# k^T v on quarters of the TensorE array, with a new order of the front

## The chip, the cores and the metric

The kernel runs on one core of a Trainium2 chip. The metric is the device time of one execution in microseconds, the median of three runs. The kernel takes float32 inputs and returns a float32 output; inside, most products work on 16-bit floats and sum in 32 bits.

## The reference

Linear attention with an ELU feature map feeds a layer of eight experts, whose routing weights come from eight rounds of Sinkhorn scaling. Shapes: batch 8, 8 heads, 576 positions, head size 64; 4608 tokens of 512 features; 8 experts with 1024 hidden features.

```
phi(x) = where(x > 0, x, exp(x) - 1) + 1
kv  = einsum('bhsd,bhse->bhde', phi(k), v)      # the products that are changed
z   = sum over s of phi(k)
num = einsum('bhsd,bhde->bhse', phi(q), kv)
den = einsum('bhsd,bhd->bhs', phi(q), z) + 1e-6
x   = num / den, heads side by side: (4608, 512)

P = exp(x @ w_gate - max); eight times: P /= row sums; P /= column sums; P *= N / E
out = sum over e of P[:, e] * (relu(x @ w1[e]) @ w2[e])
```

## The kernel before

**A plan of tasks.** The kernel doesn't emit its instructions as it goes through the loops. It adds tasks to a plan (`_Plan.add`), each with an engine, a duration, the tasks that it depends on, and the buffers that it takes from pools and hands back. `_Plan.run` then emits the tasks. Where a list of (task, engine) pairs is given, that list decides the order; after its end the planner picks by start time and priority. The list is the string `_FRONT`: a number is a task, the letter its engine (p TensorE, a ScalarE, d VectorE, g GpSimd, s SyncE, m a transfer, n nothing). A task that two engines could do (`{"dve": 0.43, "act": 0.37}`) is given to one of them by the letter. Each engine works through its own instructions in the order in which they were emitted.

**The front.** `_FRONT` covers the attention of all 8 batches and, between its pieces, the work of the first expert that can already be done. Attention goes by step: one step is one batch and one group of four heads, 16 steps in all. A step holds the 128 partitions as two halves of 64: the lower half has heads of one pair, the upper of the other; `r` is the head within the pair, `j` runs over 9 positions of 64 rows. For each step `att`

- loads k, q and v (line 380: GpSimd's queue, but for the very first k, which goes by SyncE's), 3 buffers of each; the planner reckons with 8 loads under way in GpSimd's queue;
- computes phi(k) into `t` (exponential on ScalarE, L390; two operations on VectorE, L394 and L398), and phi(q) into `tq` in the same way (L447, L450, L454);
- multiplies `t` with v on TensorE into `kv_ps` (`f_kv`, L413) - this is what the change touches. The tile `vv` holds v of head 0, a block of ones, and v of head 1, so that one product gives kv and z together;
- copies the useful part of `kv_ps` into `kvz` (L340 on ScalarE, L342 on VectorE, one copy for each head of the pair);
- transposes `tq` on TensorE (L439), copies the result (`qpT`), multiplies it with `kvz` for the denominators (`att`, L470) and the numerators (`num_ps`, L470), and forms the quotient by logarithm and exponential (L483, L488 on ScalarE) and a product on VectorE (L498) into `xT`.

Of the 128 x 192 result of a half-array product, rows of head 0 use the columns of v0 and ones, rows of head 1 the columns of ones and v1.

**Around it.** At the start TensorE has 46 products on zeros (`warm`, L590) to fill its waits. The first expert's first layer writes `hq` (L684), its second `ye` (L932), both by groups of four products of 512 columns. After every second batch `logits` (L515) computes the gate's values, 36 products of 8 columns. When the last are there, the Sinkhorn rounds run on VectorE (L541 to L565) with one small product on TensorE in each (`R`, L556). Beside them, blocks of sums and differences of `xT` (L726 to L731, on VectorE or GpSimd, into `acc` and later into `xst`) and of weights (`W`, L982) are made, from which later units compute with seven products in place of eight (L810, L1050); they are stored to `xd` by SyncE's queue, and an `xst` buffer is free again when its store has landed. For experts 1 to 7 the order of TensorE's work is fixed by a chain of dependencies.

## Time and profile before

| what | value |
|---|---|
| time, median of 3 runs | 964.44 us (964.11 to 965.62) |
| time of the profiled execution | 967.64 us |
| its span, first to last instruction | 965.6 us |
| busy TensorE, VectorE, ScalarE, GpSimd | 98%, 81%, 60%, 19% |
| mean granted TensorE clock | 0.997 |
| 18 products of a kv step (L413) | 16 steps of 0.92 us or a little less |
| group L413 | x288, 243 ns each, 14.7 us busy |

The profile is one execution, taken apart by engine. A line of the timeline or of the chain gives start and length in microseconds, the engine, the line of the kernel and the tile written and read. TensorE's instructions are pipelined: the length of a single product contains its latency, so the distance between two starts says more than the length. The profiled execution is 2.0 us longer than its span, and 3.2 us above the median of the runs.

### The profile page before, as it was taken

Reading aid. Unit: us, or ns where it says so; the run is one execution under the profiler, and the core shown is the slowest. Engines: PE = TensorE matmul, PEld = TensorE weight load, DVE = VectorE, ACT = ScalarE, POOL = GpSimd, SP = SyncE. Lnnn points to the kernel's source line nnn. Section 1 sums busy time; section 2 is a strip of 40 time slices with the busy share of each in tenths; the row PEclk is TensorE's granted clock in tenths of the full one; section 3 lists DMA queues with packets and bytes.
Section 4 is the critical chain, followed back from the end, with each engine's and each line's share of the span. In section 5 each row is a group of like instructions: output and inputs, shape, how many; then the busy total and the mean of one; then the engine's idle time right before and its main releaser. Section 6 shows DMA issues by size and latency. Waiting matters only on the chain.

```text
span 965.6 us, 21108 instructions
## 1 busy us (share of the span) xinstructions
PE 950.3 (98%) x8576; PEld 805.2 (83%) x8576; DVE 782.0 (81%) x1474; ACT 579.3 (60%) x1031; POOL 184.6 (19%) x238
## 2 busy tenths in 40 slices
PE   7999999999999999999999999999999999999998
PEld 4555568888888888888888888888888888888886
DVE  6899899778888788878887888878887888877775
ACT  6898856666655555555555555555555555555553
POOL 6435021452111121111112111111112111111110
PEclk9999999999999999999999999999999999999999
DMA  9999382225323352262226322272226322235654
GB/s 220 244 249 209 106 235 80 53 88 121 98 77 100 99 120 78 89 153 78 77 78 133 105 72 72 72 159 71 76 75 139 100 77 77 78 99 164 165 163 111
DMA packets 45681, 112.52 MB, mean 117 GB/s; under 512 B 4368, under 2 KB 25616, under 8 KB 45584
## 3 DMA queue, kind: packets, MB, share of 16 engines
q1 hardware_dynamic: 21056, 75.57, 24.0%
q0 software_dynamic: 24128, 35.07, 19.8%
q8 instruction: 67, 1.10, 0.5%
q10 hardware_dynamic: 400, 0.52, 0.2%
q14 instruction: 30, 0.25, 0.1%
HBM read 119.69 MB, written 17.69 MB: 142 GB/s over the span
## 4 chain that ended last, share of the span: by engine, by line
PE 95%; DMA 2%; DVE 2%; issue 0%; ACT 0%; POOL 0%; DVEq 0%; ACTq 0%; POOLq 0%
PE ye L1050 36%; PE hq L810 24%; PE R L810 12%; PE Zye L810 6%; PE Zye L1050 6%; PE ye L932 4%; PE hq L684 3%; DMA vv<-in_v_dram 2%; PE kv_ps L413 1%; PE att L439 1%; PE att L470 1%; PE num_ps L470 1%; DVE wt L549 0%; PE att L515 0%; PE yw L590 0%
## 5 line engine op out<-in xcount | busy, mean ns | idle before, releaser
L1081 DVE SCALAR_TENSOR_TENSOR acc<-ye,P_sb,acc 128x256 f32<-128x256 f32 x620 | 268.8, 479 | 124.7 <-PE ye L1050 123.1
L810 PEld LDWEIGHTS <-W 128*128 128x128 f16 x2144 | 209.9, 98 | 25.5
L1050 PEld LDWEIGHTS <-S 128*128 128x128 f16 x1984 | 194.1, 98 | 22.8 <-DVE S L1021 0.4
L1091 POOL TENSOR_TENSOR acc<-acc,st 128x256 f32<-128x256 f32 x124 | 88.1, 730 | 601.0 <-ACT st L1088 594.5
L1050 PE MATMUL ye<-T,S 128*128 128x256 f16 x1488 | 192.8, 273 | 0.1
L810 PEld LDWEIGHTS <-w 128*128 128x128 f16 x1608 | 157.5, 98 | 19.8 <-issue 1.1
L1050 PEld LDWEIGHTS <-h 128*128 128x128 f16 x1584 | 154.9, 98 | 18.0
L845 ACT ACTIVATE h<-hq 128x512 f16<-128x512 f32 x134 | 80.2, 598 | 130.6 <-PE hq L810 127.7
L810 PE MATMUL R<-xs,W 128*128 128x256 f16 x1008 | 151.2, 273 | 0.0
L810 PE MATMUL hq<-xs,W 128*128 128x256 f16 x1008 | 151.2, 273 | 0.0
L810 PE MATMUL hq<-xs,w 128*128 128x256 f16 x1008 | 140.9, 273 | 0.3 <-DVE h L848 0.3
L825 ACT COPY Zye<-hq 128x512 f32<-128x512 f32 x134 | 77.7, 580 | 47.6 <-PE hq L810 47.3
L842 ACT ACTIVATE h<-Zye 128x512 f16<-128x512 f32 x134 | 80.0, 597 | 43.0 <-PE Zye L810 42.7
L848 DVE CUSTOM_DVE_ANT_0 h<-R,s 128x512 f16<-128x512 f32 x126 | 86.5, 686 | 13.0 <-ACT s L832 13.0
L1021 DVE TENSOR_TENSOR S<-h 128x1024 f16<-128x1024 f16 x124 | 86.1, 694 | 11.2 <-ACT h L845 11.2
L1088 ACT ACTIVATE st<-Zye,P_sb 128x256 f32<-128x256 f32 x124 | 53.1, 471 | 69.1 <-PE Zye L1050 68.2
L832 ACT COPY s<-hq 128x512 f32<-128x512 f32 x126 | 73.5, 583 | 32.3 <-PE hq L810 31.8
L848 DVE CUSTOM_DVE_ANT_0 h<-hq,s 128x512 f16<-128x512 f32 x126 | 86.6, 687 | 5.1 <-PE hq L810 2.6
L810 PE MATMUL Zye<-xs,w 128*128 128x256 f16 x504 | 75.6, 273 | 0.0
L839 ACT COPY s<-R 128x512 f32<-128x512 f32 x126 | 74.6, 592 | 1.2 <-PE R L810 0.7
L1050 PE MATMUL ye<-w,h 128*128 128x256 f16 x528 | 68.4, 273 | 0.0
L1050 PE MATMUL Zye<-w,h 128*128 128x256 f16 x528 | 68.4, 272 | 0.0
(125 smaller groups left out, 1013.8 us busy)
## 6 DMA issues: line engine op xcount, KB each, us to landing
xs<-xd SPq DMA_DIRECT2D x63, 896.0 KB, 4.6
kin<-in_k_dram POOLq DMA_DIRECT2D x15, 576.0 KB, 8.3
out_dram<-acc SPq DMA_DIRECT2D x67, 128.0 KB, 2.4
w<-in_moe_w_dram POOLq DMA_DIRECT2D x16, 512.0 KB, 7.7
w<-in_moe_w_dram POOLq DMA_DIRECT2D x7, 1024.0 KB, 13.1
vv<-in_v_dram POOLq DMA_DIRECT2D x16, 288.0 KB, 9.0
qin<-in_q_dram POOLq DMA_DIRECT2D x16, 288.0 KB, 7.6
xd<-acc SPq DMA_DIRECT2D x5, 512.0 KB, 3.6
```

Of the source, the lines that this page charges most:

```text
L810: nc.tensor.matmul(dst[:, p, :], lhsT=lhs(p, c), rhs=rhs(c), start=(first and p == 0 and c == 0), stop=(c == 1), skip_group_check=True)
L825: nc.scalar.copy(out=Zt[1], in_=gX["tile"])
L832: nc.scalar.copy(out=gs2["tile"], in_=gX["tile"])
L839: nc.scalar.copy(out=gs5["tile"], in_=gR["tile"])
L842: nc.scalar.activation(out=hd(0, 0), in_=Zt[1], func=AF.Relu)
L845: nc.scalar.activation(out=hd(1, 0), in_=gX["tile"], func=AF.Relu)
L848: nc.vector._custom_dve(TENSOR_ADD_SAT, out=dst, in0=ps, in1=sb, s0=3.0e38, s1=0.0)
L1021: nc.vector.tensor_tensor(out=Sx[:, i], in0=a0, in1=a1, op=op)
L1050: nc.tensor.matmul(bank(g_)[:, s, :], lhsT=lhs(s, kk), rhs=rhs(kk), start=(new and s == 0 and kk == 0), stop=(kk == 3), skip_group_check=True)
L1081: nc.vector.scalar_tensor_tensor(out=dst(), in0=bank(g_)[:, s, :], scalar=P_sb[:, gg, e:e + 1], in1=dst(), op0=ALU.mult, op1=ALU.add)
L1088: nc.scalar.mul(out=gst["tile"], in_=bank(g_)[:, s, :], mul=P_sb[:, gg, e:e + 1])
L1091: nc.gpsimd.tensor_tensor(out=dst(), in0=dst(), in1=gst["tile"], op=ALU.add)
```

## The change

Two things are changed. First, each half-array product (64 rows x 128 columns of weights, 192 columns streamed) becomes two quarter-array ones (64 x 64, 128 columns streamed): head 0 with v0 and ones into partitions 0 to 63, head 1 with ones and v1 into partitions 64 to 127. A step has 36 products and 36 weight loads in place of 18 and 18. The columns of `kv_ps` that were never read are no longer written. Second, the duration of the task in the plan is 0.53 where it was 0.85, and `_FRONT` is another list, somewhat longer, that was searched with that duration.

```
     for j in range(NJ):
         for hh in range(2):
             s = slice(64 * hh, 64 * hh + 64)
-            nc.tensor.matmul(gkv["tile"][:, hh, 0:3 * D].rearrange("p (r d) -> p r d", r=3),
-                             lhsT=gt["tile"][s, j, :, :].rearrange("p r d -> p (r d)"), rhs=gin["v"]["tile"][s, :, j, :],
-                             start=(j == 0), stop=(j == NJ - 1))
+            for r in range(2):
+                nc.tensor.matmul(gkv["tile"][64 * r:64 * r + 64, hh, 64 * r:64 * r + 2 * D].rearrange("p (r d) -> p r d", r=2),
+                                 lhsT=gt["tile"][s, j, r, :], rhs=gin["v"]["tile"][s, r:r + 2, j, :],
+                                 start=(j == 0), stop=(j == NJ - 1))
...
-        tkv = fadd(("pe", 0.85), f_kv, deps=[tk, tin["v"], tza], acq=[gkv], use=[gin["v"], gt], prio=pr, cfg=1)
+        tkv = fadd(("pe", 0.53), f_kv, deps=[tk, tin["v"], tza], acq=[gkv], use=[gin["v"], gt], prio=pr, cfg=1)
```

The list begins and ends like this:

```
-    48s 49m 1n 2p 3p 52g 53m 4p 50g 51m 5p 6p 78g 79m 7p 8p 76g 77m 9p 10p 126g 127m 54a 55d 11p 12p 80g 81m 13p 14p
+    48s 49m 1n 2p 3p 50g 51m 4p 52g 53m 5p 6p 78g 79m 7p 8p 76g 77m 9p 10p 126g 127m 54a 11p 12p 80g 81m 13p 14p 15p
...
-    1691d 1695p 1719n 1725a 1692d 1697p 1693d 1696a 1727a 1700p 1698d 1699d 1730p 1694d 1701a 1705p 1731d 1702g
+    2070d 1708p 1645g 1706d 1732p 1707d 1734p 1647g 1703a 1709d 1736p 1733a 1710d 1704g 1711p 1729d 1735a 1737a 2065n
+    2066g 1740p 1712d
```

What the new order moves, engine by engine, as the instructions stand in the built programs:

- GpSimd's first loads are q, v, q, k, k, v, k, q, v, q and then the first piece of w1 (eleventh); before they were v, q, q, k, k, v, q and the first piece of w1 (eighth).
- The differences of `xT` (L726 to L731) stay at 13 on GpSimd and 23 on VectorE in all, at other places. Ahead of the Sinkhorn rounds VectorE makes the first pair (L726, L727) of two late blocks, GpSimd the L729 of one and then the first pair of the third; before, GpSimd made the first pair of the second.
- Between the first two L556 products, TensorE had 12 products of `ye` and 12 of `hq` (4 of them L810); now it has two `Zye` of L652 and four `R` of L810 besides. Between the sums `gs` that these products read, VectorE now has three more subtractions (L729, L731 twice).
- After the end of the list, the planner's own picks follow from the new durations; the order of experts 1 to 7 on TensorE is the chain's as before.

## The prediction

> **What bounds the kernel now.** I read the page first. Its part 1 and its chain say that TensorE (PE) carries the end.

> ```profile
> span 965.6 us, 21108 instructions
> PE 950.3 (98%) x8576; PEld 805.2 (83%) x8576; DVE 782.0 (81%) x1474; ACT 579.3 (60%) x1031; POOL 184.6 (19%) x238
> PE 95%; DMA 2%; DVE 2%; issue 0%; ACT 0%; POOL 0%; DVEq 0%; ACTq 0%; POOLq 0%
> ```

> So a microsecond of PE work taken out counts in full wherever PE has no wait around it. The windows view splits the part that the change touches (its columns are length, then busy time and count of PE, PEld, DVE, ACT and POOL, then granted clock, DMA share, GB/s).

> ```profile
> 0.00:28.00 28.00, 21.30 (x159) 10.91 (x161) 18.19 (x31) 18.84 (x22) 16.11 (x28) 1.00 1.05 219
> 28.00:120.00 92.00, 89.61 (x827) 52.54 (x823) 85.36 (x139) 80.91 (x112) 33.74 (x43) 1.00 0.90 203
> 120.00:131.00 11.00, 9.05 (x72) 4.83 (x69) 10.61 (x20) 4.61 (x9) 3.94 (x5) 1.00 0.85 264
> 131.00:134.50 3.50, 3.50 (x14) 1.86 (x13) 3.33 (x10) 1.66 (x3) 0.00 (x0) 0.51 1.18 187
> ```

> Three stretches. Up to 28 us the loads decide (DMA share 1.05), and PE fills its waits with the `warm` products. From 28 to 120 us PE is busy 89.6 of 92 us, with DVE (85.4) and ACT (80.9) close behind: PE leads, with little room. Around 130 us something else happens: PE idles 2 us and then has a granted clock of 0.51 for 3.5 us.

> Next the timeline of PE, for the step that is changed and its nearest relative (start, length, operation; 128 columns a product in the second line).

> ```profile
> 34.92 0.92 PE L413 MATMUL kv_ps<-vv,t 64*128 64x192 f16 x18
> 16.60 0.66 PE L439 MATMUL att<-ident,tq 128*128 128x128 f16 x9
> ```

> One product takes 243 ns in the first (its group's mean) and 219 ns in the second, nearly all of it latency: what counts is the distance from one to the next. Nine transposes of 128 columns: (0.66-0.219)/8 = 55 to 56 ns apart, so a column costs 0.435 ns. One after the other, eighteen half-array products of 192 columns would take 18x0.084 = 1.5 us. They take 0.92, (0.92-0.243)/8 = 84 ns for each pair: **the two halves of the array already work side by side.**

> Last the chain of waits, for the steady front and for the stall at 130 us.

> ```profile
> 68.71 0.85 PE kv_ps L413 x18
> 69.55 0.97 PE ye L932 x4
> ...
> 72.13 0.88 PE att L515 x36
> ...
> 126.88 3.17 DVE wt L549
> ...
> 130.58 0.39 PE R L556 x2
> 130.97 0.81 PE R L810 x4
> 131.78 1.71 PE ye L932 x4
> 133.49 0.85 PE Zye L810 x4
> ```

> [...] The `wt` product of VectorE took 3.17 us here, against 0.69 for the same line at 122.12. In the same time GpSimd ran two subtractions:

> ```profile
> 127.25 1.17 POOL L726 TENSOR_TENSOR xst<-xT 128x512 f16<-128x512 f16 x1
> 128.37 1.16 POOL L727 TENSOR_TENSOR xst<-xT 128x512 f16<-128x512 f16 x1
> ```

> VectorE ended 0.5 us after GpSimd's second. PE, waiting for the Sinkhorn sum behind it, stood 1.95 us, and then four `ye` products took 1.71 us, twice their 0.86.

> **The products.** Removed: 16 steps of 18 products of 192 columns. Added: 16 steps of 36 products of 128 columns, four to a position j, one in each quarter of the array. The third of the old output that nobody read (v0 against head 1, v1 against head 0) is no longer streamed. If the four quarters work side by side as the two halves do, positions follow at the 56 ns of the transposes: 8x0.056+0.219 = 0.67 us for a step against 0.92, **0.25 us less**. [...] From the other side, thirty-six in single file take 35x0.056+0.219 = 2.18 us, +1.26 a step; from below, the 128 columns must be streamed, so more than 0.25 isn't to be had. I take the near end, since the pairs of L413 show side-by-side work with products of the same kind and data.

> How much of it lies on the path: of 16 steps the chain of waits has 13 behind 27 us. The first three (7.86, 15.69 and 20.41 us) stand in the load-bound stretch with `warm` products around them and give nothing. One of the 13, at 95.29, starts after a wait for `xT` of VectorE, and other steps are followed by a wait for the copies of ACT; DVE is busy 93% of 28 to 120 us, so part comes back as waits. I count 12: 12x0.25 = **-3.0 us** (bounds 0 and 16x0.25 = 4.0 at this duration).

> Weight loads double to 36 a step, each of 64 columns. A half-array load takes 94 ns, and in `att` L515 thirty-six full-width loads and their products of 8 columns pass in 0.88 us, 24.4 ns each. Cost zero, hidden behind the streaming; without that cover it is the second rival.

> **The order.** The front's list is new, so three places want a price.

> *Opening.* GpSimd now issues the first q before the first v. Loads land one slot apart (about 1.45 us), so the first kv step moves from 7.86 to about 9.3 us. Behind it in the old trace stand sixteen `warm` products (3.6 us) until the transposes at 12.17, which cover it: zero; 1.4 us if they didn't. The first piece of w1 falls behind three more loads, some 4.4 us, from landing at 18.2 to 22.6; its first product ran at 23.99. Zero, with 1.4 us to spare.

> *Middle.* Copies, stores and loads are shuffled among engines. Stalls of PE in the old trace: 1.58 us (26.15), 0.59 (56.8), 1.19 (94.1). I find no line that says they vanish or grow. Zero, bounds -1.5 and +1.5.

> *Sinkhorn.* Between the first and the second L556 product PE now has two `Zye` products and four `R` more: 4.75 us of work become 5.62 (0.216 us a product of 512 columns, 0.109 of 256). VectorE has three subtractions of `xst` more (0.33 us each from start to start): without the collision its old 7.25 us are 7.25-2.48 = 4.77, and become 5.77. That leaves a wait of 0.2. GpSimd's L726 and L727 now belong to the third late block, which needs a freed `xst` buffer; the old third block ran at 154.98 us, so they move out of this stretch. In their place GpSimd does one 1.27 us L729 ahead of the first sum. That can hold VectorE's `W` for up to 1.3 us; PE has 3.44 us queued there against some 2.9 that it must bridge, so up to 0.7 idle; I take 0.5. Idle: 1.95-0.2-0.5 = 1.25 us won. The half clock cost 0.37+0.85+0.41 = 1.63 us (three groups against 0.44, 0.86 and 0.44). With the idle time in two small pieces I expect none there, but count half, 0.8, as I can't see whether the timed runs had it. Together **-2.05** (bounds -3.6 and +1.0, a collision elsewhere).

> **Sum.** -3.0-2.05 = -5.05. The profiled execution took 967.64 us in all, 2.0 more than its span, and becomes 962.6; it was 3.2 above the median of 964.44, to which I apply the same difference: **959.4 us**. Own range: 956 (four steps more, whole clock loss, part of the middle's gain) to 962.9 (the order costs 1.5 instead of giving 2.05).

> [...]

> **The rivals.**

> *A floor for each product.* If the array takes no more than one product in 24.4 ns whatever its width (L515), thirty-six need 35x0.0244+0.219 = 1.07 us, 0.15 more than now; two quarters of a row half taking turns give 8x0.112+0.219 = 1.11, 0.20 more. Times 12: +1.9 to +2.4; with the order's -2.05 964.3 to 964.8. For it: L515 shows the floor with full-width products. Against: pairs of L413 are not held to single file. [...]

> *Loads on the path (slower).* A load of one quarter isn't hidden any more, and the two of a row half go one after the other at the recorded 94 ns: 188 ns a position, 8x0.188+0.219 = 1.72 us, +0.8 a step, 12x0.8 = +9.7, with the order 972.1. It decides from 108 ns a position (8x0.108+0.219 eats the 2.05 of the order), and passes 0.2% from 128 ns. For it: nothing in the trace loads quarters. Against: loads of 94 to 98 ns hide at 24.4, 56 and 84 ns so far.

> *The order brings nothing.* The products gain 3.0, but a new meeting of GpSimd and VectorE, or a load that lands late, costs 1.5: 962.9. For it: the old order, too, met one. Against: the pieces above are spread.

> **Numbers.** Forecast 0.65, new stall 0.16, floor or turns 0.10, loads 0.09. A measurement can tell about 0.2%, 1.9 us: faster is below 962.5, slower above 966.4. Faster: 0.65, half of the stall case and a little of the floor, less a margin for what I haven't priced, 0.72. Slower: loads, the worse end of turns and of stalls, 0.15. The rest, 0.13, within. The range takes in the floor and the turns: 956 to 965.

> **What would show it.** Right: L413's successor as x36 in about 0.67 us; positions 56 ns apart; `wt` near 0.69 us at every pass, no granted clock of a half around 125 to 135 us; logits of the last batch 3 to 4 us earlier than 119.66. Wrong: steps of 1.07 us (floor) or 1.7 (loads), with PEld back to back; or steps of 0.67 and new idle time of PE behind DVE or POOL.

## The result, and the profile after

The changed kernel took 960.82 us in the median of twelve runs (958.34 to 962.3), the kernel before, beside it on the same chip, 965.37 us (twelve runs, 963.67 to 969.88). The ratio is 0.995, with a 95% interval of 0.9939 to 0.9961. That is 4.55 us less by the medians; 5.05 had been forecast, and the time lies 1.4 us above the forecast 959.4, inside its range of 956 to 965. The profiled execution took 962.2 us, 1.8 more than its span, and stands 1.4 above its median. By profiles the change is thus 5.4 us, by medians 4.55; the difference is what two single executions can be off.

Lines of the code behind L413 stand three numbers higher in the changed kernel. `kv_ps` is L416, `ye` L935, the logits L518, the products of the Sinkhorn rounds L559, `wt` L552. The page of the changed kernel, the parts that answer to those of before:

```profile
span 960.4 us, 21682 instructions
PE 946.8 (99%) x8864; PEld 803.1 (84%) x8864; DVE 777.1 (81%) x1476; ACT 578.2 (60%) x1031; POOL 181.9 (19%) x236
PE 94%; DVE 3%; DMA 2%; ACT 1%; issue 0%; POOL 0%; DVEq 0%; ACTq 0%; POOLq 0%
```

PE has 288 products more (and 288 loads) and 3.5 us less to do. The chain's share of VectorE is up from 2 to 3%, that of ScalarE from nothing to 1%. The windows view, in the same four stretches and the same columns:

```profile
0.00:28.00 28.00, 22.00 (x239) 11.70 (x240) 18.30 (x32) 18.19 (x22) 16.57 (x29) 0.88 1.03 225
28.00:120.00 92.00, 88.63 (x1059) 51.24 (x1057) 83.68 (x140) 81.54 (x113) 36.98 (x47) 1.00 0.95 215
120.00:131.00 11.00, 11.00 (x70) 6.64 (x69) 10.45 (x27) 6.51 (x12) 0.78 (x1) 1.00 0.67 203
131.00:134.50 3.50, 3.50 (x36) 3.15 (x34) 3.40 (x8) 2.66 (x5) 0.00 (x0) 1.00 0.00 0
```

The last two rows are the Sinkhorn stretch: PE never waits and the clock is whole, where it had waited 1.95 us and then run 3.5 us at 0.51. The first row is the other way round: the granted clock is 0.88, where it had been 1.00. A half clock is now in the opening. The timeline of PE shows the wait ahead of it, and the changed step:

```profile
1.31 5.72 PE L593 MATMUL yw<-warm 128*128 128x512 f16 x15 [1.31 <-DVE warm L582]
9.99 1.17 PE L416 MATMUL kv_ps<-vv,t 64*64 64x128 f16 x36 [2.95 <-DVE t L400]
...
62.13 0.70 PE L416 MATMUL kv_ps<-vv,t 64*64 64x128 f16 x36
62.76 1.04 PE L935 MATMUL ye<-w,h 128*128 128x512 f16 x4
```

The step of 36 products lasts 0.70 us (0.92 before) and hands over to `ye` after 0.63 (0.85). Inside it the recorded starts of the positions are 62.212, 62.268, 62.324, 62.380: 56 ns apart, and the four products of one position start within 10 ns. Ahead of the first step PE now stands 2.95 us, waiting for `t`; from 9.44 to 16.26 us the clock is granted by half, and the step at 9.99 takes 1.17. The chain of waits, in the places that were shown of before and one that is new:

```profile
67.92 0.63 PE kv_ps L416 x36
68.55 0.97 PE ye L935 x4
...
85.10 1.66 DVE t L396
86.75 0.67 DVE xT L501
87.42 1.30 DVE tq L457
88.77 0.68 PE att L442 x9
...
118.57 0.88 PE att L518 x36
...
128.68 0.12 PE R L559 x2
```

The `ye` behind a step still costs 0.97, where a group of four takes 0.86 elsewhere in the front: these 0.11 us a step are as they were. The second product of the rounds takes 0.12 at once. New is the piece from 85 to 89 us: there VectorE is the chain, and two of its operations, `t` and `tq`, take 1.66 and 1.30 us, where each normally takes 0.75. The timelines of VectorE and then of GpSimd at such places:

```profile
7.93 0.46 DVE L453 TENSOR_SCALAR tq<-qin 128x1152 f16<-128x1152 f16 x1 [4.85 <-DMA qin<-in_q_dram]
8.31 0.75 DVE L396 TENSOR_SCALAR t<-kin 128x1152 f16<-128x1152 f32 x1
...
31.77 2.00 DVE L396 TENSOR_SCALAR t<-kin 128x1152 f16<-128x1152 f32 x1
...
85.01 1.74 DVE L396 TENSOR_SCALAR t<-kin 128x1152 f16<-128x1152 f32 x1
...
87.34 1.37 DVE L457 TENSOR_TENSOR tq<-tq,eq 128x1152 f16<-128x1152 f16 x1
...
127.03 0.67 DVE L552 TENSOR_TENSOR wt<-P_sb,Rr 128x288 f32<-128x288 f32 x1
```

```profile
30.86 1.17 POOL L729 TENSOR_TENSOR acc<-xT 128x512 f16<-128x512 f16 x1
31.97 1.16 POOL L730 TENSOR_TENSOR acc<-xT 128x512 f16<-128x512 f16 x1
...
84.50 1.44 POOL L382 DMA_DIRECT2D kin<-in_k_dram  x2
85.92 0.99 POOL L382 DMA_DIRECT2D qin<-in_q_dram  x1
86.92 1.17 POOL L734 TENSOR_TENSOR acc<-xT,acc 128x512 f16<-128x512 f16 x1
```

The first two lines of VectorE are the opening: `tq` of the first q stands ahead of `t` in VectorE's order, so `t` waits for the load of q, 4.85 us, although it reads k. This order is the smaller part of PE's wait: v, issued at 2.50 us, landed 6.9 us later, at 9.4, and the step began at 9.99. The others run beside instructions of GpSimd: meetings, as such places are called below, at which an operation of VectorE takes far longer than others of its kind. The operation at 31.77 ends at 33.77, 0.64 us after GpSimd's second subtraction; that at 87.34 ends 0.62 after the one of 86.92. Against the 0.75 us of such an operation elsewhere, these ends look as if VectorE did most of its work only after GpSimd was through. At 127 us, where `wt` had taken 3.17, GpSimd has nothing and `wt` takes 0.67.

**Where the time went.** In both kernels the last batch of logits has the same work behind it, so the span divides there. Before: logits at 119.66, then 965.6 - 119.66 = 845.9 us. After: logits at 118.41, then 842.0. The profiles give 1.25 us to the front and 3.9 to what follows. The forecast had 3.0 and 2.05. The total was nearly right, the split of these two profiles is another, and the experiments ask why.

### The profile page after: what moved, and what is told of

It is laid out like the page before. It is cut to its first block, busy times and chain, and to the rows that moved or that the text cites. A ratio compares the mean times of both kernels' runs of the same rounds, so it can differ in the third digit from the quotient of the medians.

```text
span 960.4 us, 21682 instructions
## 1 busy us (share of the span) xinstructions
PE 946.8 (99%) x8864; PEld 803.1 (84%) x8864; DVE 777.1 (81%) x1476; ACT 578.2 (60%) x1031; POOL 181.9 (19%) x236
## 4 chain that ended last, share of the span: by engine, by line
PE 94%; DVE 3%; DMA 2%; ACT 1%; issue 0%; POOL 0%; DVEq 0%; ACTq 0%; POOLq 0%
PE ye L1053 35%; PE hq L813 24%; PE R L813 12%; PE Zye L813 6%; PE Zye L1053 6%; PE ye L935 4%; PE hq L687 3%; DMA xs<-xd 1%; PE kv_ps L416 1%; PE att L442 1%; PE att L473 1%; DMA qin<-in_q_dram 1%; PE num_ps L473 1%; DVE xT L501 1%; DVE t L396 1%; PE yw L593 0%
```

## The experiments

All ratios are to the kernel before on the same chip, with a 95% interval. One per cent is 9.65 us.

**The two parts by themselves.** The first kernel has the quarter products in the old order, the second the new order with the old half-array products.

```
e1: the kernel before, with the change's lines in f_kv, old _FRONT
e2: the changed kernel, with the old lines in f_kv, new _FRONT
```

> The old order with quarter products alone. Theory A (the two parts add): a kv step takes 0.63 us in the chain in place of 0.85, 12 of 16 steps count, so -2.6 us against before, about 962.8; the stall behind the Sinkhorn sum with wt at 3.2 us and the half clock after it stay. Theory B (the old order cannot use the shorter step, since VectorE and ScalarE are as late as they were): under -0.8 us. In both, positions of the step stand 56 ns apart.

> The new order with the old half-array products. Theory A: kv steps back at 0.85 us, +2.6 us against the changed kernel, and still 2 us below before, since the Sinkhorn stretch has no collision. Theory B (the order only works with the shorter step it was searched for): as slow as before or slower, waits of PE in new places.

Measured: quarters alone 968.07 us (965.13 to 970.44), 1.0015 (1.0001 to 1.0029): no gain, rather a small loss. The order alone 964.54 us (962.01 to 968.97), 0.9983 (0.9969 to 0.9997). On the old order the products are worth nothing; on the new one they are worth the difference of 0.9983 and 0.995, 3.2 us (1.7 either way). The step takes the same 0.70 us on either order, with 56 ns between positions. In the first kernel the profile shows the first two logits 3 us earlier than before (54.4 and 68.8), the third only 0.6 (101.6). About half of the 3 us is how executions differ: two kernels further down that have the half-array products and the same instructions as before up to there (e3 and e12) show these logits at 55.7 to 55.9, 70.3 to 70.5 and 100.5 to 100.7. Against them the quarters are 1.4 to 1.6 us ahead at the first two and 0.8 to 1.1 behind at the third. Between stands this, in the timeline of VectorE, of GpSimd and of PE:

```profile
80.48 3.51 DVE L455 TENSOR_TENSOR tq<-tq,eq 128x1152 f16<-128x1152 f16 x1
```

```profile
81.09 1.17 POOL L727 TENSOR_TENSOR acc<-xT 128x512 f16<-128x512 f16 x1
82.21 1.15 POOL L728 TENSOR_TENSOR acc<-xT 128x512 f16<-128x512 f16 x1
```

```profile
84.77 0.41 PE L471 MATMUL num_ps<-qpT,kvz 128*128 128x288 f16 x2 [2.39 <-ACT kvz L340]
```

A shorter step brought VectorE's `tq` to just where GpSimd subtracts, it took 3.51 us in place of 0.75, the copies of `kvz` stood behind it, and PE waited 2.39 us for them. The old stall at the Sinkhorn rounds was there as well (`wt` 3.18 us, PE idle 1.97), but in this execution without the half clock. Nine of the twelve runs had a mean granted clock of 0.998 or less (median 968.09 us), three of 1.000 (965.36): the small loss goes with the clock.

**The meeting at the Sinkhorn rounds.** One letter of the old list is changed: GpSimd's pair of subtractions goes to VectorE, where it now runs at 131.26 us, behind the third sum.

```
-    ... 534d 842g 800p 799a ...
+    ... 534d 842d 800p 799a ...
```

> The kernel before with one pair of subtractions (L726, L727 of the second late block) given to VectorE, where it stands behind the second Sinkhorn sum, in place of GpSimd; nothing else moves. Theory A (GpSimd's pair held VectorE's wt): wt at 0.69 us, PE's wait of 1.95 us falls to about 0.2, no half clock after it: -1.75 to -3.4 us against before. Theory B (the wait has another cause, such as the clock or the transfers): wt stays at 3 us, time unchanged.

Measured: 962.32 us (961.58 to 963.28), 0.9955 (0.994 to 0.997), nearly the gain of the whole change. In VectorE's timeline:

```profile
125.19 0.66 DVE L549 TENSOR_TENSOR wt<-P_sb,Rr 128x288 f32<-128x288 f32 x1
```

No stall of PE, no half clock. So GpSimd's pair was the cause of `wt`'s 3.17 us, and the letter alone gives 4.3 us (1.4 either way), twice the term that the prediction had for this place.

**The half clock there, without the stall's removal.** Nine products on zeros, whose result nobody reads, fill the wait ahead of the second product of the rounds; the stall itself stays.

```
-            def f_c(_, gc=gc):
+            def f_c(_, gc=gc, it=it):
                 gc["tile"] = r_bank()[:, 0, 2 * E:3 * E]
+                for _ in range(9 if it == 1 else 0):
+                    nc.tensor.matmul(Zt[0].rearrange("p a b -> p (a b)"), lhsT=warm[:, 0:P], rhs=warm, start=True, stop=True)
```

> The kernel before, with 9 products on zeros ahead of the second Sinkhorn product, where PE stands 1.95 us; the wait for VectorE stays. Theory A (the half clock after it follows from PE's standing still): granted clock 1.00 after it, -1.2 to -1.6 us against before. Theory B (the half clock follows from something else, or is rare in the timed runs): under 0.5 us.

Measured: 965.0 us (963.88 to 966.04), 0.9997 (0.9985 to 1.0008). In the timeline of PE and the windows view:

```profile
126.98 2.11 PE L557 MATMUL Zye<-warm 128*128 128x512 f16 x9
129.13 0.39 PE L558 MATMUL R<-gs,ones_t 128*128 128x8 f32 x2
```

```profile
131.00:134.50 3.50, 3.50 (x35) 3.13 (x33) 3.33 (x9) 2.69 (x6) 0.00 (x0) 1.00 1.24 207
```

The clock is whole, and the median hardly moves. The interval (1.4 us faster to 0.8 slower) still holds the 0.8 us that the prediction counted for half of it, but not the 1.63 of the one profile. The clocks of the single runs say why. A half clock of 3.41 us takes 0.0018 off the mean of a run. Of the 50 runs of the kernel before that stood beside the experiments, 27 had a mean of 0.999 or more and a median of 965.0 us, 23 had 0.998 or less and 966.7: 1.6 us more, what the profile showed. All twelve runs of e12 and all six of e3 had 0.999 or more. So the low means go with PE's standing still at this place, and about half of the runs have them, as the prediction had counted; beside e12 it was 4 runs of 16, so that their median had little of it to lose.

With this kernel the stretch behind the logits can be taken apart, as the span less the start of the last logits:

| kernel | stall | half clock | last logits | rest of the span |
|---|---|---|---|---|
| before | yes | yes | 119.7 | 845.9 |
| old order, quarters (e1) | yes | no | 118.8 | 844.3 |
| old order, wait filled (e12) | yes | filled | 118.2 | 844.3 |
| old order, one letter (e3) | no | no | 118.0 | 842.2 |
| after | no | no | 118.4 | 842.0 |

The stall costs 2.1 us, the half clock, where it comes, 1.6. The column of the logits says something else: before, e12 and e3 have the same instructions up to there, and lie 1.7 us apart. What one pair of profiles tells of the front (the 1.25 us above) is no more than this scatter.

**Quarters in the old order, without meetings.** First the two longest meetings are taken out of the first kernel (two letters), then every subtraction that the list gave to GpSimd is given to VectorE (nine letters, 13 operations).

```
e5: e1 with 576g -> 576d, 842g -> 842d
e6: e1 with 563 570 576 583 584 842 844 901 958, each g -> d
```

> Quarter products in the old order, with two pairs of subtractions given to VectorE in place of GpSimd: the one that held wt behind the Sinkhorn sum (842) and the one that held tq for 3.5 us at 80 us when the quarters ran alone (576). Theory A (the quarters' gain was there and was eaten by the second meeting): the 4.0 us of 842 and 2.6 us of the products add, about 6.6 below before, clearly under the old order with 842 alone. Theory B (VectorE and ScalarE bind the front, so a shorter step gives nothing whatever GpSimd does): as fast as the old order with 842 alone, 4.0 below before.

> As the one before, with all subtractions of the list that stood on GpSimd given to VectorE. Theory A (each meeting costs VectorE more than the 0.33 to 0.42 us of doing the subtraction itself): another 0.5 to 1.5 us faster. Theory B (VectorE is the bound in the front, and thirteen more operations there, some 4.5 us, cost in full): 2 to 4 us slower than with two moved.

Measured: with two 962.07 us (960.74 to 962.61), 0.9964 (0.9953 to 0.9976); with nine 959.85 us (959.26 to 961.69), 0.9949 (0.9937 to 0.9961). The first is the same as the half products with one letter (0.9955; 0.9 us slower, 1.8 either way): without its two longest meetings, too, the old order makes at most 0.9 us of the shorter step, so the wait of 2.39 us alone isn't what ate the gain. Three shorter meetings are left there (1.96 us at 53.0, 1.3 at 90.8 and 1.4 at 92.0, each in place of 0.45). PE's idle time of over 0.1 us adds up to 9.5 us there and to 6.5 with the half products; most of the difference are waits for loads of v, 2.7 us against 0.3, which the kernel before has too (3.4). Loads that land early or late from one execution to the next are in these sums, so the medians say more here than the profiles. With all nine moved no operation of VectorE between 14 and 135 us takes over 0.25 us more than the shortest of its kind, and the kernel is as fast as the changed one, with the old order. No run has half products with all nine moved, so how much of the last 2.2 us is the quarters' and how much the letters' stays open.

**The new order: its early wait and its meetings.** Twelve products on zeros (result unread) go ahead of the very first kv step; one letter takes the meeting at 31.8 us away; ten letters take GpSimd out of all of them.

```
e4:       f_kv, ahead of its loops:
+            for _ in range(12 if n == 0 else 0):
+                nc.tensor.matmul(yw[0], lhsT=warm[:, 0:P], rhs=warm, start=True, stop=True)
e8:       555g -> 555d
e7:       555 557 563 564 577 578 585 843 900 958, each g -> d
e9:       e4 and e8 together
e10:      e4 and e7 together
```

> The changed kernel with 12 more products on zeros in PE's wait of 2.95 us ahead of the first kv step. Theory A (that wait halves the clock from 9.4 to 16.3 us, and the late first steps delay the front): clock 1.00 there, first step at full speed, -1.5 to -2.5 us against the changed kernel. Theory B (the stretch up to 28 us is bound by the loads): clock 1.00, but time within 0.5 us of the changed kernel.

> The changed kernel with all subtractions of its list that stood on GpSimd given to VectorE. Theory A (meetings at 31.8 and 87.3 us are what ate the products' gain in the front): last logits 1 to 2 us earlier, 1 to 2 us below the changed kernel. Theory B (VectorE is the bound): 2 to 4 us above the changed kernel.

> The changed kernel with its first pair of subtractions (555) given to VectorE; the pair held t L396 for 1.25 us at 31.8 us. Theory A: PE's wait of 1.0 us there shrinks by half, since VectorE now spends 0.75 us on the pair itself: -0.3 to -1.0 us against the changed kernel. Theory B (that wait is made up again before the last logits): no difference.

> The changed kernel with both cures: 12 products on zeros ahead of the first kv step, and the first pair of subtractions (555) on VectorE. Theory A (the early half clock and the meeting at 31.8 us each cost the front in full): 2 to 3 us below the changed kernel, about 0.7% below before. Theory B (one of them is made up by the other or by a wait for loads): no better than the better of the two alone (0.9934 and 0.9943 of before).

> The changed kernel with the 12 products on zeros and with all subtractions of the list on VectorE. Theory A (without the half clock, taking all meetings away pays, as in the old order): below the previous one, about 0.75% below before. Theory B (VectorE's thirteen more operations cost as much as the meetings): as the previous one or up to 1 us above.

| kernel | median, us (range) | ratio (95%) | last logits |
|---|---|---|---|
| after | 960.82 (958.34 to 962.3) | 0.995 (0.9939 to 0.9961) | 118.4 |
| e4, early wait filled | 960.37 (958.14 to 962.07) | 0.9934 (0.9916 to 0.9952) | 118.4 |
| e8, one letter | 960.19 (958.54 to 960.63) | 0.9943 (0.9931 to 0.9955) | 116.2 |
| e9, both | 960.09 (958.62 to 961.56) | 0.995 (0.9936 to 0.9963) | 117.0 |
| e7, ten letters | 960.65 (959.71 to 961.43) | 0.9951 (0.9939 to 0.9963) | 117.2 |
| e10, ten letters, wait filled | 958.59 (958.27 to 960.21) | 0.9939 (0.9927 to 0.9951) | 114.7 |

The opening of the kernel with the wait filled, in the timeline of PE:

```profile
7.17 2.75 PE L413 MATMUL yw<-warm 128*128 128x512 f16 x12
9.85 0.70 PE L418 MATMUL kv_ps<-vv,t 64*64 64x128 f16 x36
```

The step takes 0.70 in place of 1.17, and the granted clock was 0.999 or 1.0 in every run of that kernel; of the changed kernel's runs it was 0.995 or 0.996 in all but one, and that one, at 1.000, was the fastest (958.34 us). Over all these kernels, the mean was 0.999 or more in 16 of 17 runs with the wait filled (e4, e9, e10) and in 3 of 23 with the wait left (after, e7, e8). So the wait brings the half clock on, though not alone: the one exception, the profiled run of e9, has it from 12.6 to 16.0 us, behind waits of 0.46, 0.31 and 0.85 us.

That the half clock costs time isn't settled. In e8, which keeps the wait, the two runs at 1.000 took 958.5 and 958.7 us and the three at 0.996 took 960.6; but e4, with a whole clock in all six, ranges from 958.1 to 962.1. There the first step starts hardly earlier than in the changed kernel (9.85 against 9.99), the last logits are at 118.4 as well, and the gain is 1.5 us (2.1 either way): not told from nothing. Nor are the letters by themselves, although the 2.00 us operation is gone with 555. Why one meeting less doesn't show stays open. The last kernel, with both, has the lowest median of all and is faster than the kernel before by 0.49 to 0.73%; its interval overlaps that of the changed kernel.

**Columns in turn.** The loop over the head in the pair goes outermost, so neighbouring products have the same columns of the array.

```
-            for j in range(NJ):
-                for hh in range(2):
-                    s = slice(64 * hh, 64 * hh + 64)
-                    for r in range(2):
+            for r in range(2):
+                for j in range(NJ):
+                    for hh in range(2):
+                        s = slice(64 * hh, 64 * hh + 64)
```

> The changed kernel with the loop over the two column halves outermost: all products of head 0, then all of head 1, so that only the two row halves can work side by side. Theory A (the gain of the step rests on the column halves working side by side): 18 positions 56 ns apart, a step of 1.15 to 1.2 us in place of 0.70. Theory B (products of 64 columns of weights follow each other faster than 56 ns for a pair): a step under 0.9 us.

Measured: 964.41 us in the one execution, and in the timeline of PE

```profile
58.98 1.00 PE L416 MATMUL kv_ps<-vv,t 64*64 64x128 f16 x36
```

1.00 us lies between what the two theories expected, and neither was right. The rows don't name the columns, but the recorded starts fall into two series of nine pairs. Taken in the order of the program, the pairs of the first columns start at 59.060, 59.116, 59.172 and so on, 56 ns apart, and the first pair of the second columns at 59.293, when three pairs of the first are still to come (59.340, 59.395, 59.451); from there, after a first gap of 80 ns, it goes on at 56 ns to 59.764. It looks as if each half of the columns kept its own pace, and products for a free half passed those that waited for a busy one, here three pairs early. Side by side from the start, as in the changed kernel, the nine positions need 0.30 us less; twelve steps of 0.30 would be 3.6 us. This one execution lies 3.6 us above the changed kernel's median, but single executions of one kernel differ by as much, so that agreement proves nothing.

## Why the prediction was right, and where its split was wrong

**Products: the price of a step was right.** 0.67 us were expected at 56 ns a position; the profile has 56 ns and 0.70, since the first position takes some 80 ns. Against the chain's own 0.85 of before, 0.63 is 0.22 less, not 0.25.

**Products: how many steps count was wrong as a property of the products.** Twelve of sixteen, 3.0 us, fits what the two kernels on the new order show (3.2, 1.7 either way); at 0.22 us a step that is anything from seven steps to all sixteen. On the old order the same steps gave nothing (e1, and e5 against e3). The prediction had VectorE's 93% in view, but took only one step off for it, and three for the loads. What it did not see is that the other twelve, too, hang on the order of the other engines. Meetings of VectorE and GpSimd are one way in which they do, with waits for v beside them; which of them ate the gain on the old order the runs leave open.

**Opening: the cover failed, its price stays open.** The load of v came at 9.4 us, near the 9.3 of the prediction. The first step came at 9.99, because the new list also puts `tq` of the first q ahead of `t` on VectorE. The sixteen `warm` products that the old trace had behind that step no longer stood between it and the transposes, which follow at once, so they covered nothing; PE waited 2.95 us and the clock halved for 6.8 us. The prediction had moved the load and left the rest as it was in the old trace. But the transposes themselves came earlier (11.09 against 12.17), since q did, and no experiment shows that the opening as a whole costs time. The w1 part held: PE shows no wait for a load up to 140 us, and the first `hq` product now stands at 29.11 us, not at 23.99.

**Middle: taken as zero, not confirmed.** The old waits at 26 and 94 us are gone, new ones of 1.01 us (34.6), 0.78 (86.7), 0.60 (88.2) and 0.77 (98.4) have come. The order alone gives 1.6 us (1.4 either way); if the Sinkhorn stretch gives from 2.1 (the stall) to 4.3 (the one letter), opening and middle together cost 0.5 to 2.7, give or take the same 1.4. The stated bounds, 1.4 for the opening and 1.5 for the middle, come to 2.9 together.

**Sinkhorn: right mechanism, mis-sized.** The stall left whole, where 0.7 us of idle time had been kept for it: PE is busy 11.00 of 11.00 us. GpSimd's L729 (now L732) came at 119.05 as expected, but `W`, beginning beside it at 119.08, took its usual 0.68. The term of 1.25 measured 2.1 by the table, and with the half clock the profiles differ by 3.9 where 2.05 was forecast. In the median, counting half of the clock was right: 23 of 50 runs had it, at 1.6 us. That is also much of what the one letter's 4.3 us has beyond the stall. Beside it 16 of 23 runs of before had the lower clock; against the other seven (965.2 us) it gives 2.9, near the stall's 2.1.

**The total** was right in part by luck. The products' term fits. By the letter and the order alone, two errors cancel in the rest: Sinkhorn gave more than its 2.05, and the opening and the middle, taken as zero, gave that back. Both errors are of the size of the intervals, so the sum is surer than its parts.

**Floor and turns.** Four products in 56 ns are 14 ns each, well under 24.4, so that floor isn't one of the whole array: refuted. Turns are refuted as well, by 56 ns a position in place of 112. The last experiment puts one column half behind the other: 1.00 us a step, in which the second series of starts begins three pairs before the first has ended.

**Loads on the path.** A quarter load is recorded with 107 ns, a half one had 94; thirty-six of them run under positions of 56 ns, and the step takes 0.70 us, so of a price in time there is no trace here.

**The order brings nothing.** Close to what happened on the other list: e1 met a new collision that held PE for 2.4 us, and had no gain. But e5, without that collision, had none that the runs can tell either. So the rival's outcome came on the old order, not on the new, and its mechanism is at most a part of the reason.

## What to carry to other kernels

Where TensorE leads by a few per cent only, as here, time taken out of its step can come back as waits in an order that was made for the longer one; measure the shorter step on the old order and on the new, since here the two differed by all of the gain. After each new order look for VectorE's operations that are longer than others of their line, and at what GpSimd does in that moment: one letter that moved a pair of subtractions was worth nearly as much as the whole change. Compare the granted clocks of single runs, too, before a difference of medians is given to the edit. And when a load or an operation is moved in the opening, follow what stands behind it in the new order, not in the old trace, down to the clock: here a wait of 2.95 us was followed by half the clock for 6.83.

## What had not been expected of the hardware

**VectorE beside subtractions of GpSimd.** Operations of 0.67 to 0.75 us took 2.00 (31.77), 3.17 (126.88, before) and 3.51 (80.48, quarters alone), and ended 0.64, 0.5 and 0.6 us behind the last of two subtractions of GpSimd. None of them ended between the two, which follow each other without a gap. At 126.88 and 80.48 VectorE's operation is recorded as begun 0.37 and 0.61 us ahead of the first subtraction, while GpSimd was still issuing a load, and took 3.17 and 3.51 us all the same. The other way round it was seen in one place: GpSimd's L732 at 119.05, recorded 0.03 us ahead of VectorE's `W`, took 1.73 us in place of 1.17 while `W` took its usual 0.68. What decides between the two, these starts don't show. The operation at 85.01 took 1.74 us while GpSimd only issued loads. That an issue alone makes this isn't shown: in e7 the same operation, at 84.28, lies inside an issue of GpSimd (84.19 to 85.18) and takes 0.75. In e6, e7 and e10, where GpSimd has no subtraction in the front, nothing of VectorE is long between 14 and 135 us.

**Waits and the clock.** A wait of 2.95 us at 7.03 was followed by half the clock for 6.83 us, one of 1.95 at 128.6 by 3.41 us in the profile of before and by none in that of e1 (1.97 us at the same place). In the opening of e7 2.11 us were followed by 6.83 us, in that of e8 3.00 us by only 3.41. So the length of the wait alone doesn't decide it.
